# A spectral filter and a two-layer perceptron in one kernel: DMA transposes, long-row weight loads, packed small-tile products, and second-layer sums moved into the filter chain

## The chip, the cores and the metric

One core of one Trainium2 chip. The metric is device time of one execution in microseconds (us), bfloat16 in and out. Names in the profiles: PE is TensorE (matrix products), DVE VectorE, ACT ScalarE and POOL GpSimd (elementwise work), SP the queue that issues most DMAs; SBUF is the on-chip memory, PSUM the memory that matrix products are summed in, and copying a result from PSUM to SBUF is an eviction. A TensorE clock is called full when the granted clock in the records is 1.0 and half when it is 0.5. Every run quoted here computed the right result. Each run carries a state, slow when it is over 1.5% above the fastest of the same kernel. Ratios are of fast runs alone; medians and ranges are of all runs, among them slow ones in e1 (1 of 4), e6 (1 of 6), e8 (2 of 6) and e12 (1 of 4).

## The reference, cut to what matters

```python
# x: (1, 2048, 640)   w_r, w_i: (2048, 321)   w1: (640, 1536)   w2: (1536, 640)
def _A_ref(x, w_r, w_i):                       # the spectral filter
    X = rfft2(x.astype(float32), axes=(-2, -1))
    X = X * (w_r + 1j * w_i)
    return irfft2(X, s=(S, D), axes=(-2, -1)).astype(bfloat16)

def _B_ref(x, w1, b1, w2, b2):                 # the perceptron
    return gelu(x @ w1 + b1) @ w2 + b2

xn = layernorm(x)
return x + _A_ref(xn, ...) + _B_ref(xn, ...)
```

The kernel cuts the 2048 tokens into 16 tiles of 128. Both transforms are matrix products with constant tables. Names used below: `xnT` is the transposed normalised input, the right-hand side of the first layer; `gT` the first layer's output after gelu; `Wf` the frequency weights (`w_r`, `w_i`) in SBUF; the **filter chain** is, for each of eight pairs of rows, the product with `etab` (giving `Xb`), with `mtab` (giving `Y`), the complex product with the weights on VectorE (`T = Y * Wf`, then `Z` as sums and differences of `T`), small gathers (`Zs`) and the product with `ntab`. After all pairs the inverse transform (`getab`, `htab`) and the second layer are added up per tile.

## The kernel before

A small list scheduler gives every operation to an engine and fixes each engine's order from modelled times; on the chip each engine runs its stream in that order and waits on semaphores. So an instruction that waits holds back everything after it on the same engine or queue. The sync queue (SP) issues the loads in program order.

```python
DEPTH = 2                                    # weight loads in flight
few = []
def load_w(wsrc, p0, off, row, n, step):     # 16 partitions x n rows of 321 elements
    few.append(load(bass.AP(tensor=Wf, offset=p0 * WP + off, ap=[[WP, 16], [2 * KP, n], [1, 321]]),
         bass.AP(tensor=wsrc.tensor, offset=..., ap=[[128 * 321, 16], [step * 321, n], [1, 321]]),
         B_w, 16 * 642 * n, after=[wpad] + few[-DEPTH:][:1], rate=110e3))
# ... 18 such loads, then per tile c:
    ring_ops.append(K.op([("pe", 5 * mm_us(128))], pr, xt, reads=[xn, B_id], writes=[tps]))   # five transposes
    K.op([("dve", ...), ("act", ...)], pr, copy(xnT[...], tps), ...)                          # and their eviction
# ... chain, per pair: two groups of eight 64x64 matmuls (mtab), each with its own eviction to Y
    K.op([("dve", ...)], pr, T = Y * Wf)            # k = 0, 1: 1288 elements
    K.op([("dve", ...)], pr, Z = T0 -/+ T1)         # r = 0, 1: 644 elements
# ... ntab: per half pair 8 + 2 matmuls of 128 columns on the whole array
# ... after the chain, per tile c:
    K.op([("pool", ...)], 50, xo = xr + b2bc)       # residual + bias of the second layer, GpSimd
    # 24 matmuls gT x W2 and 2 matmuls htab into one PSUM tile, then DVE: out = PSUM + xo
```

## Time and profile before

| | before |
|---|---|
| time, median of 3 runs | 169.76 us (169.74 to 171.06) |
| span of the profiled execution, clock | 167.6 us, 1.00 |
| 512-column / 320-column matmul, end to end | 216 / 136 ns |
| `T` (1288 elements) / `Z` (644 elements) on VectorE | 0.82 / 0.485 us |
| one 160-KB weight load, issue to landing | 4.1 to 4.2 us, 18 loads |
| mean busy share of the 16 DMA engines, 26 to 50 us | 0.29 to 0.43 |

### The profile page before, as it was taken

Reading aid. Unit: us, or ns where it says so; the run is one execution under the profiler, and the core shown is the slowest. Engines: PE = TensorE matmul, PEld = TensorE weight load, DVE = VectorE, ACT = ScalarE, POOL = GpSimd, SP = SyncE. Lnnn points to the kernel's source line nnn. Section 1 sums busy time; section 2 is a strip of 40 time slices with the busy share of each in tenths; the row PEclk is TensorE's granted clock in tenths of the full one; section 3 lists DMA queues with packets and bytes.
Section 4 is the critical chain, followed back from the end, with each engine's and each line's share of the span. In section 5 each row is a group of like instructions: output and inputs, shape, how many; then the busy total and the mean of one; then the engine's idle time right before and its main releaser. Section 6 shows DMA issues by size and latency. Waiting matters only on the chain.

```text
span 167.6 us, 3677 instructions
## 1 busy us (share of the span) xinstructions
PE 158.1 (94%) x1493; PEld 101.2 (60%) x1493; DVE 110.9 (66%) x288; ACT 83.0 (49%) x149; POOL 39.8 (24%) x64
## 2 busy tenths in 40 slices
PE   6889997999999999998869999999999999999993
PEld 2579783545455445544535666677777777757772
DVE  4859999999995494098999059783838383711221
ACT  3389774676767799799997744110101001011000
POOL 1306223131320000000003800333333424240300
DMA  5999824443444600000099310222222222120112
GB/s 111 351 387 392 240 55 80 79 77 46 83 83 76 159 0 4 0 0 4 0 268 354 86 43 0 78 78 81 81 78 82 78 78 79 43 74 5 39 62 63
DMA packets 15146, 16.66 MB, mean 99 GB/s; under 512 B 1304, under 2 KB 13976, under 8 KB 15128
## 3 DMA queue, kind: packets, MB, share of 16 engines
q1 hardware_dynamic: 14960, 16.38, 34.0%
q8 instruction: 12, 0.20, 0.5%
q14 instruction: 6, 0.05, 0.1%
q10 hardware_dynamic: 168, 0.04, 0.1%
HBM read 13.79 MB, written 2.62 MB: 98 GB/s over the span
## 4 chain that ended last, share of the span: by engine, by line
PE 72%; ACT 10%; DVE 7%; DMA 5%; POOL 2%; SPq 1%; issue 1%
PE ps L470 71%; DMA XV<-in_A_x_dram 5%; ACT Xb L477 4%; ACT Y L477 2%; DVE stats L565 2%; ACT XV L477 2%; DVE T L578 2%; PE ps L585 1%; SPq L465 1%; ACT gT L630 1%; DVE xnT L480 1%; POOL rstd L569 1%; DVE T L603 1%; POOL ve L568 1%; ACT Zs L477 1%
## 5 line engine op out<-in xcount | busy, mean ns | idle before, releaser
L470 PE MATMUL ps<-xnT,W 128*128 128x512 bf16 (+2 forms) x360 | 59.0, 308 | 2.0 <-ACT gT L630 0.6
L470 PE MATMUL ps<-XW,gT 128*128 128x320 bf16 x384 | 55.1, 299 | 0.0
L470 PEld LDWEIGHTS ps<-XW,gT 128*128 128x128 bf16 x384 | 37.3, 98 | 14.6 <-DVE ost L783 0.5
L630 ACT ACTIVATE gT<-ps,b1col 128x512 bf16<-128x512 f32 (+2 forms) x72 | 36.8, 545 | 14.1 <-PE ps L470 13.9
L470 PEld LDWEIGHTS ps<-xnT,W 128*128 128x128 bf16 x360 | 28.0, 98 | 21.0 <-ACT gT L630 4.0
L783 DVE TENSOR_TENSOR ost<-ps,xo 128x640 bf16<-128x640 f32 (+1 forms) x17 | 13.3, 784 | 29.2 <-PE ps L470 29.2
L764 POOL TENSOR_TENSOR xo<-xr,b2bc 128x640 f32<-128x640 bf16 x16 | 22.4, 1405 | 42.6 <-DVE ost L783 42.5
L477 ACT ACTIVATE Wf<-ps 128x640 bf16<-128x640 f32 x8 | 5.6, 704 | 37.3 <-PE ps L470 37.3
L686 DVE TENSOR_TENSOR T<-Y,Wf 128x1288 bf16<-128x1288 bf16 x16 | 12.5, 824 | 8.2 <-ACT Y L477 8.2
L565 DVE BATCH_NORM_STATS2 stats<-XV 128x6 f32<-128x320 bf16 x32 | 14.9, 479 | 3.5 <-DMA XV<-in_A_x_dram 3.5
L477 ACT ACTIVATE XV<-ps 128x640 bf16<-128x640 f32 x16 | 11.1, 710 | 3.2 <-PE ps L470 3.2
L480 POOL COPY Zs<-Z 128x128 bf16<-128x128 bf16 x8 | 3.2, 402 | 39.9 <-DVE Z L691 39.9
L477 ACT ACTIVATE XW<-ps 128x640 bf16<-128x640 f32 x14 | 9.7, 703 | 5.4 <-PE ps L470 5.1
L568 POOL TENSOR_SCALAR ve<-mv 128x1 f32<-128x1 f32 x16 | 4.3, 269 | 32.6 <-DVE mv L567 32.6
L603 DVE TENSOR_TENSOR T<-T 128x256 bf16<-128x256 bf16 x64 | 11.8, 232 | 0.1
L480 DVE CAST Wf<-ps 128x640 bf16<-128x640 f32 x8 | 6.6, 822 | 6.8 <-PE ps L470 6.4
L470 PE MATMUL ps<-ntab,Z 128*128 128x128 bf16 x128 | 9.8, 220 | 1.3 <-ACT Y L477 1.3
L470 PEld LDWEIGHTS ps<-ntab,Z 128*128 128x128 bf16 x128 | 7.7, 98 | 5.0 <-ACT Y L477 2.4
L477 ACT ACTIVATE Y<-ps 128x644 bf16<-128x644 f32 x15 | 10.3, 702 | 0.2 <-PE ps L470 0.2
L751 DVE TENSOR_TENSOR Wf<-Wf 128x640 bf16<-128x640 bf16 x16 | 10.0, 667 | 0.4
L477 ACT ACTIVATE Xb<-ps 128x640 bf16<-128x640 f32 x10 | 9.1, 906 | 1.5 <-PE ps L470 1.2
L569 POOL TENSOR_TENSOR rstd<-ve,mhalf 128x1 f32<-128x1 f32 x16 | 9.4, 585 | 1.3
(43 smaller groups left out, 145.5 us busy)
## 6 DMA issues: line engine op xcount, KB each, us to landing
xr<-in_A_x_dram SPq DMA_DIRECT2D x16, 160.0 KB, 2.2
out_dram<-ost SPq DMA_DIRECT2D x15, 160.0 KB, 1.8
XV<-in_A_x_dram SPq DMA_DIRECT2D x7, 320.0 KB, 9.2
W<-in_B_w_dram SPq DMA_DIRECT2D x3, 640.0 KB, 7.0
XW<-in_B_w_dram SPq DMA_DIRECT2D x1, 1920.0 KB, 8.4
Wf<-in_A_w_r_dram SPq DMA_DIRECT2D x7, 160.5 KB, 4.2
Wf<-in_A_w_i_dram SPq DMA_DIRECT2D x7, 160.5 KB, 4.1
gtab<-c_G SPq DMA_DIRECT2D x1, 512.0 KB, 8.6
```

The source lines that it names most:

```text
L470: ins = e.matmul(o_, lhsT=lw, rhs=rh, start=st, stop=sp_)
L477: return e.activation(dst(), src(), ACT.Copy, scale=scale)
L480: return e.tensor_copy(dst(), src())
L565: K.op([("dve", 0.4)], pr, lambda e, _, c=c, h=h: e.bn_stats(stats[:, c, 6 * h:6 * h + 6], view(XV, c * D + H2 * h, [[1, H2]])), reads=[B_ ...
L568: K.op([("pool", 0.1)], pr, lambda e, _, c=c: e.tensor_scalar_add(ve[:, c:c + 1], mv[:, c, 1:2], 1e-5), reads=[B_mv], writes=[B_ve[c]])
L569: K.op([("pool", 0.6)], pr, lambda e, _, c=c: e.tensor_tensor(out=rstd[:, c:c + 1], in0=ve[:, c:c + 1], in1=mhalf[:, c:c + 1], op=ALU.pow) ...
L603: K.op([("dve", dve_us(2 * n, 2))], prf, lambda e, _, op=op, x1v=x1v, xfv=xfv, o_=o_, o0=o0, o1=o1, n=n: e.tensor_tensor(out=xfv(o_, [[2 * ...
L630: K.op([("act", act_us(s1 - s0, 1))], pr + PRIO["gelu"], lambda e, _, s0=s0, s1=s1, fc=fc, hps=hps: e.activation(gT[:, fc, s0:s1], ps(hps. ...
L686: t_ops[pair].append(K.op([("dve", dve_us(4 * KP, 2))], pr, lambda e, _, k=k, Y=Y, TB=TB, pair=pair: e.tensor_tensor(out=view(TT, TB.slot ...
L751: K.op([("dve", dve_us(D, 2))], pr + 2, lambda e, _, k=k, op=op, yo=yo, y2=y2: e.tensor_tensor(out=view(Wf, Y2 + y2.slot * 2 * D + (H2 - 1 ...
L764: K.op([("pool", pool_us(640))], 50, lambda e, _, xr=xr, xo=xo: e.tensor_tensor(out=xot[:, xo.slot, :], in0=xrt[:, xr.slot, :], in1=b2bc[: ...
L783: K.op([("dve", dve_us(H2 * len(hs)))], 95, lambda e, _, hs=hs, xo=xo, os_=os_, fps=fps: e.tensor_tensor(out=ost[:, os_.slot, H2 * hs[0]:H ...
```

## The change

Its intent: take work off TensorE (tiles 8 to 15 are transposed by DMA; the `ntab` product runs in 64-row tiles, two at a time; the two `mtab` groups of a pair become one), fill the holes of the filter chain (the second-layer sums of five tiles run inside it and wait in SBUF in float32), and load the first half of the frequency weights in long rows, so that `W2` can be placed in `W1`'s memory. The core of the diff:

```diff
+STAGED = 5
+BYPE = 8
-        def load_w(wsrc, p0, off, row, n, step): ... ap=[[WP, 16], [2 * KP, n], [1, 321]] ... (18 loads)
+        def load_w(dst, src, nbytes, rate):
+            few.append(load(dst, src, B_w, nbytes, after=few[-DEPTH:][:1], rate=rate))
+        for ri, wsrc in enumerate((A_w_r, A_w_i)):
+            for qq in range(2):                                    # four loads of 32 partitions x 10,272 bytes
+                load_w(bass.AP(tensor=Wf, offset=64 * qq * WP + ri * WR, ap=[[WP, 32], [1, WR]]),
+                       bass.AP(tensor=wsrc.tensor, offset=wsrc.offset + 32 * qq * 321, ap=[[WR, 2], [128 * 321, 16], [1, WR]]), 32 * WR * 2, 250e3)
+        ...                                                        # ten loads of reversed rows, 16 partitions, as before
+            if c < BYPE:                                           # transposes on TensorE, as before
+            else:
+                ring_ops.append(K.op([("sp", 1.25)], 50, lambda e, _, c=c, xnv=xnv: e.dma_start(
+                    xnT[:, :, 128 * c:128 * c + 128], xnv(0, [[1, D]]), transpose=True), reads=[xn], writes=[B_xnT[c]], ...))
-                    for g, k0 in enumerate((0, 1, 1, 2)): ...      # ntab: 8 + 2 matmuls on 128 rows, per half pair
+                    for k0, o in ((2, 0), (1, 128)): ...           # ntab: 16 + 8 matmuls on 64-row tiles, per pair
+                staged = c < STAGED
-                K.op([("pool", pool_us(640))], 50, ... out=xot[:, xo.slot, :], in0=xrt[:, xr.slot, :], in1=b2bc[:], ...)
+                K.op([("pool", pool_us(640))], 50, ... out=xov(0, D), in0=xrt[...], in1=b2bc[:], ..., after=all_hps if staged else [])
+                    if staged:                                     # second layer alone, into SBUF (xnT's memory, float32)
+                        st_ops += second(hs, fps, hps_ops[block_of[c]], True)
+                        K.op([("dve", dve_us(D))], 86, ... out=xov(0, D), in0=ps2(fps.slot, H2), in1=xov(0, D), op=ALU.add)
```

The staged sums live in the memory of `xnT`, so their GpSimd additions can only start after the last first-layer matmul (`after=all_hps`). The scheduler now orders the sync queue by its model too, no longer in program order, and the model is told 250 GB/s for each long load (`250e3`).

## The prediction

> **What bounds the kernel now.** I read the page first (engines, then the slices), then the table of stretches, then TensorE's timeline in the one stretch that stood out, then the chain that ended last. From the page:
>
> ```profile
> PE 158.1 (94%) x1493; PEld 101.2 (60%) x1493; DVE 110.9 (66%) x288; ACT 83.0 (49%) x149; POOL 39.8 (24%) x64
> PE   6889997999999999998869999999999999999993
> DVE  4859999999995494098999059783838383711221
> ACT  3389774676767799799997744110101001011000
> PE ps L470 71%; DMA XV<-in_A_x_dram 5%; ACT Xb L477 4%; ACT Y L477 2%; DVE stats L565 2%; ACT XV L477 2%; DVE T L578 2%; PE ps L585 1%; SPq L465 1%; ACT gT L630 1%; DVE xnT L480 1%; POOL rstd L569 1%; DVE T L603 1%; POOL ve L568 1%; ACT Zs L477 1%
> ```
>
> TensorE is full from about slice 5 to slice 39, and 71% of the chain that ended last is its matmuls. So the kernel is a TensorE stream, and time can come from two places only: fewer matmul nanoseconds, or fewer holes. The holes are in the first 6 slices and in slices 18 to 21 (the 8, 8, 6). The table of stretches (columns: stretch, length, then busy time of TensorE, its weight loads, DVE, ACT, GpSimd, clock, DMA share, GB/s) sizes the second:
>
> ```profile
> 62.00:74.00 12.00, 11.84 (x116) 5.98 (x112) 5.12 (x12) 10.48 (x17) 0.35 (x1) 1.00 0.01 1
> 74.00:90.00 16.00, 13.26 (x200) 8.09 (x199) 15.02 (x29) 14.97 (x30) 1.63 (x5) 1.00 0.38 118
> 100.00:165.00 65.00, 64.99 (x533) 45.33 (x530) 34.67 (x54) 7.68 (x11) 18.29 (x13) 1.00 0.19 63
> ```
>
> From 74 to 90 us the filter chain runs with nothing beside it. DVE and ACT are both 94% busy with PSUM evictions and the frequency product, TensorE only 83%: 2.74 us idle. From 100 to 165 us TensorE has no hole at all while ACT does almost nothing. The timeline of TensorE there (start, length, work, count, idle before and who ended it):
>
> ```profile
> 75.20 0.62 PE L470 MATMUL ps<-ntab,Z 128*128 128x128 bf16 x8
> 75.66 0.28 PE L470 MATMUL ps<-ntab,Zs 128*128 128x128 bf16 x2
> 75.78 0.62 PE L470 MATMUL ps<-ntab,Z 128*128 128x128 bf16 x8
> 76.23 0.28 PE L470 MATMUL ps<-ntab,Zs 128*128 128x128 bf16 x2
> 77.11 1.06 PE L470 MATMUL ps<-Xb,mtab 64*64 64x322 bf16 x16 [0.60 <-ACT XV L477]
> ...
> 81.40 0.47 PE L470 MATMUL ps<-Xb,mtab 64*64 64x322 bf16 x8
> 81.81 1.08 PE L470 MATMUL ps<-etab,XW 128*128 128x160 bf16 x16
> 82.82 0.47 PE L470 MATMUL ps<-Xb,mtab 64*64 64x322 bf16 x8
> ...
> 84.43 0.62 PE L470 MATMUL ps<-ntab,Z 128*128 128x128 bf16 x8 [0.48 <-ACT Y L477]
> ```
>
> The lengths contain a pipeline latency, so I use differences of starts: one half of the last chain product (8+2 matmuls) costs 75.78 - 75.20 = 0.58 us, a pair of tiles 1.16; a lone 64x64 group of eight 0.41; an etab group 1.01. Each hole is some 0.16 us longer than its bracket (76.35 to 77.11 is 0.76, shown as 0.60). Eight holes between 74 and 90 make 2.74 + 8 x 0.16 = about 3.9 us of lost issue time.
>
> **What the Trainium skill says.** (1) "TensorE: Matmul & The Clock Gate", Back-to-back issue gap, gives N/2.4 + 2.5 ns a matmul. The chain view has 15 matmuls (ten of 512 columns, five of 128) in 2.47 us; the formula gives 10 x 0.216 + 5 x 0.056 = 2.44. It agrees, and I use it. (2) "TensorEngine Tiling (Array Packing)", Key Properties: changing the tiling mode drains TensorE, and tiles run independently. Eight 64x64 matmuls of 322 columns, four at a time, should be 2 x 0.137 = 0.27 us; the trace shows 0.41, so a switch is about 0.1 us or a little more. (3) "VectorE: DVE Perf Modes", The three transpose paths: 1309 ns for a 128x128 block by DMA, and the destination is SBUF. No run here has such a transfer yet. (4) "Vector Engine (DVE) Microarchitecture Reference", 5.1 Performance modes: alignment to 4 bytes makes no difference to the packed mode. That matters because the weight rows now start at odd multiples of 321 elements. The trace agrees in a similar place: the pair of subtract/add operations L751, one writing backwards from an odd element, takes 0.89 us for both, when undisturbed. So I leave the frequency product at 0.82 us.
>
> **The change part by part.**
>
> (a) Tiles 8 to 15 are transposed by DMA. This removes 8 groups of five transposes from TensorE. In the chain each stands as 0.28 us beside full work, so 8 x 0.28 = 2.24 us off the bound. It also removes 8 evictions of 0.49 us from DVE, which was 97% busy from 28 to 52 us (23.35 of 24).
>
> (b) The last chain product in 64-row tiles: 24 matmuls for 20, but two run at a time. My estimate: 16 of 128 columns in pairs 8 x 0.056 = 0.45, 8 of 64 columns in pairs 4 x 0.03 = 0.12, two switches 0.2, makes 0.77; if 24 weight loads limit it, some 0.9. I take 0.86, so 0.30 off 1.16, x8 = 2.4 us.
>
> (c) The two 64x64 groups of a pair become one of 16: 0.82 becomes 4 x 0.137 + 0.13 = 0.68, and one switch back (0.1) goes where they stood apart, as most did. About 0.15 to 0.2 x 8, less the ones that were adjacent: 1.0 us.
>
> (d) The second-layer sums of five tiles move into the chain: 120 of the 384 matmuls of 136 ns, 16.3 us of filler. This removes no TensorE work. The order of the built kernel shows that now every unit of the chain, without exception until the last pair, has 5 to 8 filler matmuls (about 1.08 us) ahead of the next; two banks are kept for the first layer, so a filler does not wait for the chain's banks. The chain grows to 82 x 0.216 + 100 x 0.136 + 8 x (1.0 + 0.7 + 0.86) = about 52 us. DVE and ACT have about 8.5 us of work per pair there (two Xb 0.9, two Y 0.7, two products 0.82, two Z 0.49, gathers 1.3, two XV 0.7), plus gelu (16 x 0.69) and five staged additions of 0.82: 83 us of 104. So neither is the bound on average, and the 3.9 us of holes can close. I credit 2.2: the order is fixed from modelled times, and GpSimd now makes eight additions of 1.4 us among the last pairs. At 105 us one such addition stretched two DVE operations from 0.89 to 2.08 us. I expect 1.7 us of holes to remain or to be made anew.
>
> (e) A longer lead of normalisation over folding. In the head TensorE waits 0.78 us at 26.5 and 0.39 at 27.8 for tiles 6 and 7. By the order, DVE's normalisation of tile 7 comes about 1 us earlier: 0.8 us.
>
> (f) Frequency weights in long rows, W2 in three parts into W1's place. Loads; before, the last weight load is issued at 53 us and the first product starts at 58.1, waiting for ACT and not for a DMA. Worth nothing by itself. W2 can only land once the first layer has read W1; its first two thirds can come early, the last third has some 4 us of work ahead of it, about one landing. I charge 0.5 us for this and for the denser stretch of inverse transforms of the staged tiles, where DVE has two operations per tile more than TensorE covers.
>
> Sum: 2.24 + 2.4 + 1.0 + 2.2 + 0.8 - 0.5 = 8.1 us. 169.76 - 8.1 = 161.6 us. What comes after the chain is a full TensorE stream in both kernels, so what is saved earlier is saved at the end.
>
> **Rivals.** (R1) DVE becomes the bound in the chain: staged additions, two more small gathers per pair, and GpSimd's additions slowing it. For it: DVE and ACT at 94% from 74 to 90. Against it: the chain now has 52 us instead of 40 for that work. It would eat (d) and leave 164 to 165. (R2) The DMA transposes are slow or hold up the sync queue: they wait for DVE in the same in-order queue as the weight loads, and the first frequency product waits for both. Eight of 1.3 to 5 us each are spaced by DVE's 2.4 us a tile; if one takes over 5, the product starts late and first-layer blocks 4 and 5 starve: 164 to 170. Against it: DMA engines are under half busy from 28 to 60 us. (R3) The holes close completely and the head gains more, because DVE is relieved: 157 to 159. (R4) A packed product gains nothing because weight loads bind: 2.4 us lost, 164.
>
> **Range and chances.** TensorE's removed work, a + b + c = 5.6 us (3.3%), is off the bound whatever the holes do; that alone gives 164.1. Only R2, or R1 and R4 together, undo it. I say 161.6 us, 158.8 to 165.2 in 8 of 10; faster by over 2% (under 166.4) 0.92, within 2% 0.07, slower 0.01.
>
> **What would show it.** (a) 40 instead of 80 transposes, and no wait of TensorE for a DMA'd xnT. (b) ntab groups of 24 with starts 0.8 to 0.9 us apart. (c) Groups of 16 of about 0.7 us. (d) TensorE at 9 in every slice of the chain, idle there under 2 us, DVE and ACT at 75 to 85%. (e) the 512-column matmuls start about 1 us sooner than 27.8. Wrong if TensorE waits for DVE's product, for a DMA transpose or for W2 in sum over 4 us, or if DVE's 1288-element product takes 1.4 us instead of 0.82.

## More of the kernel before

The experiments ran in three batches, in which the kernel before had medians of 170.40, 170.38 and 170.21 us, so some tenths of a us between batches say nothing.

In the list of DMA issues (out<-in, queue, count, KB each, median us from issue to landing) of the kernel before:

```profile
Wf<-in_A_w_r_dram SPq DMA_DIRECT2D x7, 160.5 KB, 4.2
Wf<-in_A_w_i_dram SPq DMA_DIRECT2D x7, 160.5 KB, 4.1
```

and in the timeline of the sync queue of the same kernel (start, us, what):

```profile
22.54 13.17 SPq L465 DMA_DIRECT2D Wf<-in_A_w_r_dram  x8
36.68 16.75 SPq L465 DMA_DIRECT2D Wf<-in_A_w_i_dram  x9
53.48 0.45 SPq L465 DMA_DIRECT2D htab<-c_H  x1
```

With two loads in flight the sync queue does nothing but wait for weight loads from 22.5 to 53.5 us. That costs nothing here, because nothing else has to be issued from it then.

## The result

The changed kernel takes **186.35 us** (185.55 to 187.13, four runs); the kernel before, in the same rounds, 170.41 us (169.74 to 171.28). The ratio is 1.093 (95% interval 1.085 to 1.101): slower by 9%, where 161.6 us had been predicted. Ratios here are the mean time of one kernel's fast runs over that of the other's of the same rounds, so not quite the ratio of the medians that I quote. All outputs are right.

The page of the changed kernel: engines, three of the slices (a slice is 4.6 us), and the chain that ended last by engine.

```profile
PE 157.4 (85%) x1485; PEld 98.1 (53%) x1485; DVE 125.3 (68%) x294; ACT 80.8 (44%) x158; POOL 41.6 (22%) x62
PE   6789999910299999899999077999999899999994
DVE  4759999900396837595959999567889968361222
PEclk9999999985569999999999855699999999999999
PE 46%; DMA 24%; DVE 13%; SPq 8%; ACT 6%; issue 1%; DVEq 0%; ACTq 0%
```

There are two gaps. In slices 9 to 11 TensorE and VectorE are both all but empty, and DMA, 5% of the chain before, is now 24% of it. In slice 23 TensorE is empty while VectorE is full, and it is not full again before slice 26. With each gap the clock falls to about half, for three slices. I call them hole A and hole B.

**Hole A.** The chain that ended last, in order of time (start, us, what), shows what leads up to it:

```profile
12.98 14.12 DMA Wf<-in_A_w_r_dram
...
27.12 8.76 DMA Wf<-in_A_w_r_dram
...
36.55 12.37 DMA xnT<-T
...
49.62 5.71 PE ps L472 x23
```

Two weight loads take 14 and 9 us (the first one's packets start only at 17.8 us, when earlier loads end), and only at 36.5 us does the sync queue get to issue the first DMA transpose, which needs 12.4 us. VectorE's next normalisation waits for the transpose, and TensorE for VectorE. VectorE's waits (waited for: us in all, times, longest):

```profile
DVE T L576 <- DMA xnT<-T: 12.5, 2, 12.1
```

TensorE then restarts at 49.6 us after 11.94 us of idleness. The table of stretches (stretch, length, busy time of TensorE, its weight loads, VectorE, ACT, GpSimd, then clock, DMA share, GB/s):

```profile
34.00:36.00 2.00, 2.00 (x14) 0.94 (x13) 2.00 (x11) 1.70 (x3) 0.58 (x2) 1.00 0.13 56
44.00:46.00 2.00, 0.00 (x0) 0.00 (x0) 0.00 (x0) 0.00 (x0) 0.00 (x0) 0.50 0.12 51
50.00:56.00 6.00, 5.74 (x24) 2.26 (x21) 5.47 (x22) 2.02 (x4) 1.58 (x4) 0.66 1.24 120
```

A DMA share of 0.13 and 0.12 is two engines of sixteen. The records of the single packets agree: 10,272 bytes in about 386 ns each, and packet time over elapsed time is 1.9 to 2.1. The two engines deliver 51 to 56 GB/s, and the other fourteen do next to nothing. (Shares above 1 occur where the records of transposes overlap; I draw nothing from those.) After the hole 512-column matmuls take 427 instead of 216 ns.

**Hole B.** VectorE, then GpSimd, then TensorE of the changed kernel around 100 us (start, us, engine, line, operation, count, idle before and who ended it):

```profile
97.29 2.77 DVE L688 TENSOR_TENSOR T<-Y,Wf 128x1288 bf16<-128x1288 bf16 x2
100.10 3.17 DVE L693 TENSOR_TENSOR Z<-T 128x644 bf16<-128x644 bf16 x2
103.19 2.02 DVE L688 TENSOR_TENSOR T<-Y,Wf 128x1288 bf16<-128x1288 bf16 x1
105.13 1.36 DVE L482 COPY Zs<-Z 128x2 bf16<-128x2 bf16 x1
```

```profile
97.64 8.82 POOL L779 TENSOR_TENSOR xnT<-xr,b2bc 128x640 f32<-128x640 bf16 x5 [4.94 <-PE ps L472]
106.42 5.25 POOL L779 TENSOR_TENSOR xo<-xr,b2bc 128x640 f32<-128x640 bf16 x3
```

```profile
106.64 1.04 PE L472 MATMUL ps<-ntab,Z 64*128 64x128 bf16 x16 [5.04 <-DVE Zs L482]
```

As soon as the first layer ends, eight GpSimd additions run back to back for 14 us. Beside them two `Z` operations take 3.17 us instead of 0.97, and a copy of two elements per partition takes 1.36 us. TensorE waits 5.04 us for that copy.

What had been predicted to show, and did: 40 instead of 80 transposes; the `ntab` group of 24 takes 0.67 us where the clock is full and nothing waits; the `mtab` group of 16 takes 0.68 us; a `T` that starts at an odd element still takes 0.82 us; and from 26 to 30 us TensorE is now busy 3.89 us instead of 3.09. The prediction's own sign of being wrong came as well: it named waits of TensorE for VectorE's product or for a DMA transpose of over 4 us in sum, and there are 11.9 us in hole A alone.

### The profile page after: what moved, and what is told of

The parts are those of the page before. It is cut to its first block, busy times and chain, and to the rows that moved or that the text cites. A ratio compares the mean times of both kernels' runs of the same rounds, so it can differ in the third digit from the quotient of the medians.

```text
span 185.2 us, 3687 instructions
## 1 busy us (share of the span) xinstructions
PE 157.4 (85%) x1485; PEld 98.1 (53%) x1485; DVE 125.3 (68%) x294; ACT 80.8 (44%) x158; POOL 41.6 (22%) x62
## 4 chain that ended last, share of the span: by engine, by line
PE 46%; DMA 24%; DVE 13%; SPq 8%; ACT 6%; issue 1%; DVEq 0%; ACTq 0%
PE ps L472 46%; DMA Wf<-in_A_w_r_dram 12%; SPq L467 7%; DMA xnT<-T 7%; DMA Wf<-in_A_w_i_dram 5%; DVE Z L693 4%; DVE T L688 4%; ACT Wf L479 1%; ACT gT L632 1%; ACT Xb L479 1%; DVE xnT L806 1%; SPq L594 1%; ACT Zs L479 1%; DVE Zs L482 1%; DVE Zs L481 1%
## 5 line engine op out<-in xcount | busy, mean ns | idle before, releaser
L472 PE MATMUL ps<-W,gT 128*128 128x320 bf16 x384 | 59.6, 310 | 1.4 <-DVE xnT L806 1.3
L472 PEld LDWEIGHTS ps<-W,gT 128*128 128x128 bf16 x384 | 37.7, 101 | 18.0 <-DVE xnT L806 2.3
L779 POOL TENSOR_TENSOR xo<-xr,b2bc 128x640 f32<-128x640 bf16 x11 | 16.4, 1498 | 34.7 <-DVE ost L799 34.7
L472 PE MATMUL ps<-gtab,T 128*128 128x128 bf16 x80 | 7.2, 225 | 11.9 <-DVE T L605 11.9
L576 DVE TENSOR_SCALAR T<-XV,mv,rstd 128x640 bf16<-128x640 bf16 x16 | 7.0, 440 | 13.0 <-DMA xnT<-T 12.5
L479 ACT ACTIVATE Zs<-Z 128x128 bf16<-128x128 bf16 (+1 forms) x29 | 6.0, 277 | 15.0 <-DVE Z L693 15.0
L693 DVE TENSOR_TENSOR Z<-T 128x644 bf16<-128x644 bf16 x16 | 11.7, 770 | 0.1
L472 PE MATMUL ps<-ntab,Z 64*128 64x128 bf16 x128 | 5.8, 239 | 5.8 <-DVE Zs L482 5.0
L482 DVE CAST XV<-ps 128x640 bf16<-128x640 f32 x8 | 6.6, 821 | 5.5 <-PE ps L472 5.5
L779 POOL TENSOR_TENSOR xnT<-xr,b2bc 128x640 f32<-128x640 bf16 x5 | 8.8, 1792 | 4.9 <-PE ps L472 4.9
```

Source lines behind the costliest of these rows:

```text
L472: ins = e.matmul(o_, lhsT=lw, rhs=rh, start=st, stop=sp_)
L479: return e.activation(dst(), src(), ACT.Copy, scale=scale)
L482: return e.tensor_copy(dst(), src())
L576: norm_ops.append(K.op([("dve", 0.36)], pr, lambda e, _, c=c, xnv=xnv: e.tensor_scalar(out=xnv(0, [[1, D]]), in0=view(XV, c * D, [[1, D]]) ...
L693: K.op([("dve", dve_us(2 * KP, 2))], pr, lambda e, _, TB=TB, Z=Z, r=r, op=op: e.tensor_tensor(out=view(Zb, Z.slot * 4 * KP + r * KP, [[2 * ...
L779: K.op([("pool", pool_us(640))], 50, lambda e, _, xr=xr, xov=xov: e.tensor_tensor(out=xov(0, D), in0=xrt[:, xr.slot, :], in1=b2bc[:], op=A ...
```

## The experiments

**Theory.** Hole A comes from the source pattern of the long loads: its outermost dimension is 2, so the load runs on two engines. The Trainium skill says so: "DMA: Bandwidth & Descriptors", section Why a DMA increments its semaphore by 16 and not by 1, has a transfer use the largest number up to 16 that divides the slowest dimension (other than 1) of both patterns. Here that is 32 in SBUF and 2 in DRAM. Hole B comes from the GpSimd additions: "SBUF — State Buffer", section Who interferes with whom, has a VectorE instruction with two SBUF inputs contend with a GpSimd instruction that reads SBUF, over a pair of ports that only one of the two can hold at a time. **Rivals.** The loads are slow because they are large; the DMA transposes are slow in themselves; the kernel is only late, so that everything slides into everything else.

The first four kernels undo one cause or both.

**e1_wf16**: each long load cut into two of 16 partitions, source outermost dimension 16. Rows are as long as before.

```diff
-   load_w(AP(Wf, ap=[[WP, 32], [1, WR]]), AP(wsrc, ap=[[WR, 2], [128 * 321, 16], [1, WR]]), 32 * WR * 2, 250e3)
+   for lo in range(2):
+       load_w(AP(Wf, + 16 * lo * WP, ap=[[WP, 16], [1, WR]]), AP(wsrc, + 16 * lo * 321, ap=[[128 * 321, 16], [1, WR]]), 16 * WR * 2, 250e3)
```

> Each of the four long-row weight loads (32 partitions, source written as 2 x 16 rows of 10,272 B) is split into two of 16 partitions; nothing else changes. Theory A (two-engine loads): the DMA records show two engines busy for these loads (51 to 57 GB/s from 30 to 38 us), the transposes wait behind them, and TensorE loses 12.2 us plus about 2 us at half clock. Then the loads should land in 2 to 4 us, the 12 us hole should go, and the time fall by about 14 us to 172 us. Rival (the DMA transposes are slow in themselves, or the in-order sync queue is the trouble): the hole stays within 3 us of its size and the time stays above 182 us.

Measured: 175.84 us (173.57 to 176.35), ratio to before 1.026 (1.016 to 1.036). Hole A is gone. In the sync queue's timeline of this kernel the first transpose is now issued 8.4 us sooner:

```profile
28.14 1.31 SPq L595 DMA_TRANSPOSE xnT<-T  x1
```

It lands after 4.1 us instead of 12.4. Hole B stands as it was (5.0 us of TensorE waiting for `Zs`). A wait of 2.3 us at 60 us is new, with 3.4 us of half clock after it: the last weight load, issued at 54.4 us, lands at 58.4, and the first `T` starts at 58.6. (The profile puts this wait of VectorE down to ACT here, and to the load in e2.)

**e2_wf16_nopool**: e1, and the GpSimd additions of the staged tiles taken away. TensorE adds the bias with two matmuls per tile (a constant matrix of 1/128 times the broadcast bias), VectorE's staged addition reads the bfloat16 residual itself, and the additions for later tiles wait until the chain is over.

```diff
-   K.op([("pool", pool_us(640))], 50, xo = xr + b2bc, after=all_hps if staged else [])
+   if not staged:
+       K.op([("pool", pool_us(640))], 50, xo = xr + b2bc, after=ipc_ops)
+   # in second(), for staged tiles: two matmuls mean x b2bc into the same PSUM tile
-   K.op([("dve", ...)], 86, staged = PSUM + xo)
+   K.op([("dve", ...)], 86, staged = PSUM + xr, after=all_hps)
```

> The split loads, and in addition no GpSimd addition during the chain: b2 of the five staged tiles is added by two 320-column matmuls per tile with a constant 1/128, the residual is read in bf16 by the staged DVE addition, and the additions of the later tiles wait for the chain's end. If both causes are separate and additive: 186.4 - 14 (loads) - 10 (collisions, with their half clock) + 1.4 (ten matmuls) = about 163 us. If the second hole has another cause (DVE overloaded anyway): 170 to 173 us, like the run with split loads alone.

Measured: 164.55 us (164.06 to 165.05), ratio 0.964, clock 1.00. Both holes are gone, and the kernel is faster than before. The largest remaining hole of TensorE is 2.5 us at 60 us. VectorE's waits name its cause (waited for: us in all, times, longest):

```profile
DVE T L693 <- DMA Wf<-in_A_w_i_dram: 3.6, 1, 3.6
```

**e3_nopool**: the changed kernel with only the GpSimd additions taken away, as in e2; the long loads stay.

> Only the GpSimd additions taken out of the chain, the slow loads kept. Theory B (GpSimd's additions hold up DVE's two-tensor operations: T 1.4 us instead of 0.82, Z 1.6 instead of 0.49 between 97 and 111 us): T and Z return to 0.82 and 0.49 us, the hole of 5.2 us at 101.6 us and its half clock go, the time falls by 8 to 10 us to 177 us; the 12 us hole at 37 us stays. Rival (DVE has simply too much work there): the operations get faster but the hole shrinks by less than half, 182 to 185 us.

Measured: 177.53 us (176.60 to 177.95), ratio 1.039. Hole A stays (TensorE waits 11.6 us), hole B goes, and the means of `T` and `Z` return to 0.83 and 0.49 us. So each hole has its own cause: the loads cost 10.5 us with the additions in (changed kernel against e1) and 13.0 without (e3 against e2); the additions cost 8.8 us with the long loads in and 11.3 without. They do not quite add: 10.5 + 8.8 = 19.3, and both together give 21.8.

**e4_bype16**: the changed kernel with all sixteen tiles transposed on TensorE (`BYPE = 16`); the long loads stay. It asks whether the transposes are the cause.

> All sixteen transposes on TensorE again, the slow weight loads kept. If the slow loads hurt only by keeping the transposes waiting: the hole at 37 us goes (minus 14), 2.2 us of transposes come back, and the first product may wait some us for the weights: 174 to 178 us. If the loads hurt by the weights being late: a hole appears at the first product instead and the time stays above 182 us.

Measured: 184.25 us (183.94 to 186.47), ratio 1.084: almost nothing regained. TensorE no longer waits for transposes, but VectorE's waits show where the time went:

```profile
DVE T L688 <- DMA Wf<-in_A_w_i_dram: 9.1, 1, 9.1
```

The transposes were victims. Take them away, and the late weights themselves stop the chain, later.

**e7_colsplit**: the control for the rival "large loads are slow". As many loads of the same size as in e1, but cut by columns, so that the source's outermost dimension stays 2.

```diff
+   for half in range(2):
+       load_w(AP(Wf, + WR // 2 * half, ap=[[WP, 32], [1, WR // 2]]), AP(wsrc, + WR // 2 * half, ap=[[WR, 2], [128 * 321, 16], [1, WR // 2]]), ...)
```

> A control for the split loads: the changed kernel with each long-row load cut in two by columns (32 partitions x 2568 elements) instead of by rows (16 x 5136). Number and size of the loads are the same as in the faster run, only the source's outer dimension stays 2. If the outer dimension of 2 is what leaves two engines: the records show two engines busy again, the hole before 50 us stays and the time is 183 to 188 us. If the size or the number of loads was the reason: 173 to 177 us as with the split by rows.

Measured: 187.85 us (187.20 to 188.59), ratio 1.103, as slow as the change itself. In its table of stretches:

```profile
30.00:34.00 4.00, 4.00 (x27) 2.05 (x27) 4.00 (x18) 3.02 (x5) 1.21 (x4) 1.00 0.12 49
```

Two engines again, 49 GB/s. By their traces e1 and e7 have the same order of operations on VectorE, ACT, GpSimd and the sync queue, so the scheduler's order is no rival here either. The outermost dimension decides, not the size.

**e6_depth6**: e2 with six instead of two weight loads in flight, to close its last hole (`DEPTH = 6`).

> The run with split loads and no GpSimd additions in the chain, and in addition six weight loads may be in flight instead of two. In that run the first product still waited 3.6 us for the last weight load, and TensorE lost 2.6 us at 59.7 us. If the two-deep gating of the loads is why, that hole goes and the time falls from 164.6 to about 162 us. If the loads land no sooner (the transposes and loads share the in-order sync queue), it stays within 1 us of 164.6.

A miss. Measured: 174.91 us (174.09 to 176.72), ratio 1.026. The list of DMA issues of this kernel and TensorE's waits:

```profile
xnT<-T SPq DMA_TRANSPOSE x8, 7.5
```

```profile
PE ps L473 <- DVE T L609: 4.0, 2, 3.1
PE ps L473 <- DMA xnT<-T: 3.3, 1, 3.3
```

With more weight loads in flight the transposes land after a median of 7.5 us instead of 3.8 in e2, and TensorE waits for them between 40 and 50 us, with half clock after it. The weight loads slow down too, from 4 or 5 us each to about 7. The built order differs a little as well.

**e8_staged0**: e6 with no tile staged (`STAGED = 0`).

> The run with six loads in flight, without staging (no tile's second-layer sum is put aside in SBUF). Measures what staging itself is worth once nothing disturbs it; 52 instead of some 100 second-layer matmuls still find room in the chain in the built order. The prediction credited 2.2 us to filler; staging also costs ten matmuls for b2 (1.4 us) and five DVE additions. Expected: between 1 us faster and 3 us slower than the run with staging.

Measured: 176.21 us (174.04 to 177.28), ratio 1.030, 1.3 us slower than e6. As the transposes' holes dominate both, I take no value for staging from this pair; e11 below was made for it.

**e9_bype16**: e6 with all transposes on TensorE (`DEPTH = 6`, `BYPE = 16`).

> The run with six loads in flight, with all sixteen transposes on TensorE. By the prediction's step (a), 40 transposes of 56 ns come back: 2.2 us slower than the run with eight DMA transposes. If DMA transposes are hidden but TensorE had slack anyway: the same time. If they cost something themselves: faster.

Measured: **163.93 us** (163.80 to 164.25, six runs), ratio 0.962 (0.960 to 0.965). This beats both kernels. Its slices show no gap after the start (one 7 among the 9s), and no clock loss (the last row, the clock, is full in every slice):

```profile
PE   6889999999999999999999999999799999999993
DVE  3659999999996394967679879689999382832221
PEclk9999999999999999999999999999999999999999
```

Against e6 it is 11 us faster. Against e2 it takes back 2.24 us of transposes on TensorE and takes the same time within the noise (ratio 0.962 against 0.964, of which the interval is 0.958 to 0.970); the two also differ in `DEPTH`, and no run has split loads with `DEPTH = 2` and all transposes on TensorE. So no run shows the DMA transposes to be worth anything here: either the weights come late (e2), or the transposes do (e6).

The last three runs start from these two, to price single parts where nothing else disturbs.

**e10_pooladd**: e9 with the GpSimd additions put back.

> The kernel of e9 (163.93 us: short-row weight loads, six loads in flight, all transposes on TensorE) with the eight GpSimd additions of the staged tiles put back. Here no hole of the head is left to mix with them, so this prices the collisions alone. Theory (GpSimd additions stretch VectorE's two-operand work in SBUF while eight of them run back to back after the first layer): three holes of TensorE of 1 to 5 us around the end of the first layer, half clock after them, 171 to 176 us. Rival (the additions only hurt because the head had already made the kernel late): under 166 us and no hole over 1 us.

Measured: 172.38 us (171.89 to 173.46), ratio 1.013: the additions cost **8.45 us**, though the kernel is not late. This is net: in their place e9 has ten matmuls for the bias, 1.4 us of TensorE, and with them another built order. GpSimd starts at 83.9 us now, the end of the first layer, and the same hole comes with it. TensorE's waits:

```profile
PE ps L472 <- DVE Zs L482: 5.1, 1, 5.1
```

Single durations from the records of both kernels, for the VectorE operations that ran beside a GpSimd addition and those that did not:

```
              T alone   T beside an addition        Z alone   Z beside an addition
after         827 ns    820, 832, 2020, 2025 ns     486 ns    1570, 1572, 1677, 1678 ns
e10           828 ns    819, 833, 2019, 2027 ns     485 ns    1568, 1571, 1678, 1679 ns
```

Each stretched operation is 1.1 to 1.2 us longer, whatever its length, and ends a fixed time after an addition has ended: 0.35 us for `Z`, 0.69 for `T`. So it waits for the addition under way, rather than run at a lower rate; the additions wait in turn (1.64 to 2.05 us each, 1.40 undisturbed). The two short `T` had started before the addition. For operations with two SBUF inputs the trace agrees with the skill's page. The copy of two elements that TensorE waits for has one SBUF input, and it waited too: 1.36 us, ending 0.03 us after an addition.

**e11_staged0**: e9 with no tile staged.

> The kernel of e9 with no tile staged: all second-layer sums run after the chain, as in the kernel before. Prices the staging (the prediction's 2.2 us of closed holes) where nothing else disturbs it. Staging worth what was predicted: 165.5 to 166.5 us, with TensorE's holes of about 3 us in all back between the last first-layer matmul and the end of the chain. Rival (DVE and ACT bind the chain whatever filler there is, staging worth nothing): 163.5 to 164.3 us.

Measured: 172.64 us (171.23 to 173.17), ratio 1.013. I had expected 165.5 to 166.5. Staging is worth **8.7 us** here (net of the ten bias matmuls, which e11 does without), four times what was predicted. TensorE in this kernel, and two stretches:

```profile
95.22 1.26 PE L473 MATMUL ps<-W,gT 128*128 128x320 bf16 x8 [0.98 <-ACT Xb L480]
...
102.00 0.63 PE L473 MATMUL ps<-ntab,Z 64*128 64x128 bf16 x16 [1.79 <-ACT Zs L480]
102.44 0.30 PE L473 MATMUL ps<-ntab,Zs 64*128 64x64 bf16 x8
103.66 1.65 PE L473 MATMUL ps<-getab,XV 128*128 128x160 bf16 x16 [0.92 <-DVE XV L483]
```

```profile
100.00:106.00 6.00, 2.60 (x42) 1.48 (x40) 3.13 (x7) 1.98 (x5) 3.52 (x4) 0.82 0.09 26
106.00:112.00 6.00, 5.07 (x39) 2.98 (x40) 5.12 (x9) 1.84 (x4) 2.61 (x3) 0.50 0.29 93
```

No hole is longer than 1.8 us, but together they leave TensorE 2.60 us busy of 6; the clock falls to half at 103.8 us, within this stretch, and stays there for 10.2 us. e8, also without staging, shows the same from 108.4 us, with no hole over 1.3 us just before. It fits that a chain with less TensorE work of its own needs the filler more; no run tests this by itself.

**e12_ring**: e6 with the transposes issued from ACT's queue, and five loads in flight (six does not build).

> Like e6 (short-row loads, no GpSimd additions for staged tiles, eight DMA transposes; 174.91 us, transposes landing a median 7.5 us after issue), with five instead of six weight loads in flight (six does not build here) and the transposes issued from ACT's queue instead of the sync queue, so that they are not behind the weight loads of the same queue. Theory (the transposes waited in the queue behind those loads): median landing falls to about 3 us, TensorE's holes of 3.3 and 3.7 us between 40 and 50 us go, about 165 us, with ACT paying some 10 us of issue in the head where it is half busy. Rival (they share the same DMA engines, whichever queue they come from): landing stays at 6 us or more, the holes stay, 172 us or more.

Measured: 167.83 us (165.65 to 168.15), ratio 0.982 (0.976 to 0.988). Its profiled execution took 168.15 us and is labelled slow, being just 1.5% above the fastest; two fast runs took as long (167.69 and 167.98), so I read the landings only. Neither side was right. In the list of DMA issues:

```profile
xnT<-T ACTq DMA_TRANSPOSE x8, 9.0
```

Issue plus time to landing of the first five transposes, from the records:

```
e1    28.1+4.1   31.7+4.1   34.2+3.6   36.1+2.6   38.5+6.4
e6    29.9+6.2   33.7+8.8   36.1+8.9   40.2+9.4   43.1+8.8
e12   27.9+6.8   31.0+7.4   33.2+9.5   35.7+10.2  39.2+8.6
```

A transpose is no quicker once it is on its way from another queue, so its place in the queue did not make it slow. The DMA engines, shared with five or six weight loads in flight, are the likely reason; no run shows that by itself. But it leaves up to 4.5 us sooner, because it no longer stands behind loads that wait, and the 7 us probably came from this. Since e12 also has five loads in flight instead of six and another built order, the split of those 7 us is not settled.

## Why the prediction was wrong

It expected -8.2 us and +15.9 came. Its steps, against what the runs showed:

| step | predicted | measured |
|---|---|---|
| (a) transposes by DMA | -2.24 | TensorE's part held (40 fewer); no net gain shown: e9 without them takes the same as e2 with them |
| (b) `ntab` in 64-row tiles | 0.86 us a pair, -2.4 | 0.67 us a pair, some -3.9 off TensorE's work |
| (c) one `mtab` group | 0.68 us | 0.68 us |
| (d) staging | -2.2, with 1.7 us of holes left | filler alone -8.7 (e9, e11), its GpSimd additions +8.45 (e9, e10) |
| (e) head | -0.8 | 26 to 30 us: TensorE busy 3.89 instead of 3.09 us |
| (f) weights in long rows | "Worth nothing by itself", +0.5 with the rest | +10.5 (e1) to +13.0 (e2, e3) |

The rows (b), (c) and (e) are times of groups and stretches, not of the kernel; no run takes one of them out. e11 has all three, but neither filler nor DMA transposes, and at 172.64 us it is no faster than the kernel before (ratio 1.013, 1.009 to 1.017).

**The step that failed first is (f).** "Worth nothing by itself" rested on when the old loads were issued and landed, and did not ask how the new ones would run. The number of engines was within reach: the pattern `[[WR, 2], ...]` in the diff says two. Four loads of 321 KB are 1.3 MB; at the 54 GB/s that the changed kernel then showed they take 24 us, and the scheduler's model, by which the transposes were placed behind them, had 1.3 us for each. Rival R2 came near ("hold up the sync queue"), but was played down because "DMA engines are under half busy from 28 to 60 us". That was a mean over sixteen engines of another kernel's loads. A mean of 0.13 can be two engines that are full.

**The second is a term of (d).** The prediction had seen the collision (one addition, 0.89 to 2.08 us) and put eight of them into "1.7 us of holes to remain or to be made anew". By its own number eight such stretches of 1.2 us are 9.5 us of VectorE, in a chain where VectorE's result is what TensorE waits for; e10 measured 8.45 us. (That the two lie so near is partly chance: e10's time went into holes of 5.1, 1.3 and 0.7 us and 13.7 us at half clock.) It had also judged VectorE by its average load ("83 us of 104"), which says nothing about a queue of additions that all start at the same moment, when the last first-layer matmul frees `xnT`.

**The third is the worth of the filler**, under-sized by four: it counted the closed holes and not the half clock that a sparse chain would bring. (The 2.2 us were credited against the holes of the kernel before; the 8.7 us are against a chain that (b) and (c) had already shortened.) So (d) as written comes out at nothing: 172.38 with staging and additions (e10), 172.64 without either (e11).

R1 (VectorE becomes the bound) happened, for 14 us of the chain. R4 did not: the packed product gained more than predicted. With both repaired the kernel is at 163.93 (e9) to 164.55 us (e2), inside the predicted range. That does not confirm the sum: no run shows a gain from (a), while (b) and the filler of (d) were under-sized. It is in part luck.

What stays open: how much of e6's slowness is the shared DMA engines and how much the sync queue; and what (a) would bring if neither transposes nor weights were late.

## What to carry to other kernels

Before a DMA is called hidden, read the slowest dimension of both its patterns, work out bytes over the rate of that many engines, and list what stands behind it in the same queue. When work is handed to an idle GpSimd, ask when all of it becomes ready at once, and what VectorE does in SBUF at that moment: here a colliding operation waited until the addition under way had ended. When a stream is thinned out, price its filler with the clock that it keeps up, not only with the holes that it closes.

## What the Trainium skill lacked or had wrong

- "VectorE: DVE Perf Modes", The three transpose paths, gives 1309 ns for a block of 128x128 by DMA. For 128x640 from SBUF to SBUF the runs show 2.6 us at best and 13.5 at worst, with medians of 3.8 to 9.0 us depending on the weight loads in flight, and at least 1.20 us in the issuing queue for each. An issue time for such a transpose I found on no page.
- "SBUF — State Buffer", Who interferes with whom, is right about the collision, but has no size for it in a chain: 0.49 us became 1.57 to 1.68, 0.83 became 2.02, and eight additions cost the kernel 8.45 us.
- "TensorE: Matmul & The Clock Gate", Why this matters for your kernels, asks for no idle gap over about 3 us between bursts. That was not enough: with no gap over 1.8 us, but TensorE busy 3.09 us of the 5.8 before, the clock fell to half for 10.2 us (e11). And of two gaps of 2.3 and 2.5 us in the same place one was followed by 3.4 us of half clock (e1), the other by none (e2). The same page tells of micro-idles that do this in another kernel, without a number for how much idleness it takes.
- "TensorEngine Tiling (Array Packing)", Key Properties, names the drain at a change of tiling mode without a cost; 24 matmuls in 64-row tiles with their changes of mode took 0.67 us.
